# One-bank PSUM tiles and a modelled instruction order in an attention kernel with experts

## The chip, the cores and the metric

The kernel runs on one core of one Trainium2 chip. The metric is the device time of one execution in microseconds (us), lower is better. The time before is the median of three executions, 242.1 us (241.87 to 242.47). A profile is one execution taken by the hardware profiler; its span runs from the first to the last instruction, 238.4 us here, in an execution of 240.09 us.

The engines are called TensorE (PE in the profile, PEld for its weight loads), VectorE (DVE), ScalarE (ACT), GpSimd (POOL) and SyncE (SP). Each takes its instructions in program order and waits for other engines by semaphores.

## The reference

```python
# attention over 32 memory slots; batch 8, heads 8, seq 576, head_dim 64
a = exp(phi - max(phi, axis=2)); a = a / (sum(a, axis=2) + 1e-9)
k_m = einsum('bhsm,bhsd->bhmd', a, k)
v_m = einsum('bhsm,bhsd->bhmd', a, v)
scores = (q @ k_m.transpose(0, 1, 3, 2)) / sqrt(64)
attn_out = softmax(scores) @ v_m                     # (b, h, s, d)

# then a dense block and one expert per token; x is (4608, 512), 8 experts, F = 512
x = attn_out.transpose(0, 2, 1, 3).reshape(4608, 512)
y_dense = relu(x @ w1_dense) @ w2_dense
logits = x @ w_gate
e = argmax(logits); gate = softmax(logits)[e]
y = y_dense + gate * (relu(x @ w1[e]) @ w2[e])
```

## The kernel before

One batch is 576 tokens, and eight batches are worked off. The kernel never forms x. It folds the memory values into the first weight matrix (vw = v_m times w1, for the dense block and for one expert), so that the hidden layer is the attention weights A times vw. The expert is chosen once for a batch, from the mean of the gate products; if any token wants another, a branch at the end corrects it. In the profiled execution that branch is not taken.

Every piece of work is a named step, and a text gives the order in which the steps are put into the program: `name:batch/engine`. A step is taken up by whichever engine it runs on, and each engine's program is the sequence of its own steps in that text. In the middle of the run the order before is this, for every batch alike:

```
... e0:2 e1:2 o0:1 z:2 rz:2 yd1:1 kv:2 kvm:2 ye1:1 T:2 vTc:2/V Y1:1/A kTc:2/A q0:2 o1:1 qT0:2/V q1:2
yd2:1 vg:2 qT1:2/A ye2:1 vgc:2 pc:2 Y2:1/V choose:2 o2:1 w1:2 w2:2 yd3:1 s0:2 ET0:2 ye3:1 s1:2 ET1:2
Y3:1/A fd:2 vd0:2/V o3:1 vd1:2/V Z0:2 yd4:1 ln0:2 Z1:2 ye4:1 ln1:2 inv0:2 Y4:1/V A0:2 inv1:2 o4:1
A1:2 hd0:2 Hd0:2/A ... hd3:2 Hd3:2/A pg:2 gB:2/A fe:2 ve0:2/A ve1:2/V he0:2 He0:2 ... he3:2 He3:2
Lphi:4 yd0:2 Lv:4 ye0:2 Lk:4 Lq:4 Y0:2/V ...
```

What the steps are:

- L...: loads. `Lq`, `Lk`, `Lv`, `w1`, `w2`, `Lw1d`, `Lw2d` are issued by GpSimd and turn fp32 into fp16 on the way; `Lphi` and the staged keys and values of batch 0 are issued by SyncE.
- `e0`, `e1`: exp of phi (ScalarE). `z`, `rz`, `kv`, `kvm`, `T`, `vTc`, `kTc`: the memory keys and values, normalised, transposed and copied out as vT and kT.
- `q0`, `q1`, `qT0`, `qT1`: transposes of q on TensorE and their copies.
- `s`, `ET`, `Z`, `ln`, `inv`, `A`: scores, exp, sums, 1/sum by exp(-ln), and the attention weights A.
- `vg`, `vgc`, `pc`, `choose`: gate products of the memory values, their sum, and the expert; `w1`, `w2` then load the expert's weights at an address read from it.
- `fd`, `vd` and `fe`, `ve`: the fold with the dense and the expert's first matrix, and the copies to fp16.
- `hd`, `Hd` and `he`, `He`: hidden products (four of each per batch) and relu; `He` also multiplies by the gate `gB`, which `L`, `mxeq`, `ex`, `gates`, `pg` make.
- `yd`, `ye`, `Y`, `o`: second products of five token chunks, dense and expert into one sum, copy out, and store.

The parts that the change touches:

```python
big = ctx.enter_context(tc.tile_pool(name="big", bufs=3, space=bass.MemoryType.PSUM))
sml = ctx.enter_context(tc.tile_pool(name="sml", bufs=1, space=bass.MemoryType.PSUM))
# every tile of both is [128, 2, 512] fp32: two banks of PSUM; 3 + 1 tiles are all eight banks
# ... cut: "inp" holds 3 batches of q, k/v and phi; "y" tiles: NKEEP = 4

def fold(vt, w):
    p_vw = big.tile([128, 2, 512], F32, tag="big", name="p_vw")
    for j in range(NJ):
        for a in range(2):
            nc.tensor.matmul(p_vw[M * j : M * j + M, a, 0:F],
                             lhsT=vt[64 * a : 64 * a + 64, j],
                             rhs=w[64 * a : 64 * a + 64, j], start=True, stop=True)
    return p_vw

@step("ve0", "ve1")
def _(b, g, e):
    # ... cut: vwe is allocated
    copy(e, out=st[b]["vwe"][:, g], in_=st[b]["pve"][:, g, 0:F])

def second(b, c, half):
    # ... cut
    if half == 0:
        if c % 2 == 0:
            x["py2"] = big.tile([128, 2, 512], F32, tag="big", name="p_y")
        x["p_y", c] = x["py2"][:, c % 2]       # two chunks share one tile
    # ... cut: four products (eight of half size in the last chunk) into p_y

@step("z")      # "att" holds z, the keys/values (second bank), T, vg, pc and L of a batch
def _(b, i, e):
    x["att"] = sml.tile([128, 2, 512], F32, tag="sml", name="p_att")
    # ... cut

@step("vg")
def _(b, i, e):
    att = st[b]["att"]
    for a in range(2):
        for j in range(NJ):
            nc.tensor.matmul(att[M * j : M * j + M, a, 400 : 400 + E],
                             lhsT=vT[b][64 * a : 64 * a + 64, j],
                             rhs=wg[64 * a : 64 * a + 64, j], start=True, stop=True)
```

Of the kernel before, what the change touches and what calls it, by code (L numbers as in the profile page):

```python
# [10 lines left out]
F32 = mybir.dt.float32  # L11
# [8 lines left out]
cones:0 Lphi0:0 Lphi1:0 Lwg:0 cid:0 ciota:0 cblk:0 ciotac:0 stage0:0 stage1:0 stage2:0 stage3:0  # L20
stage4:0 stage5:0 warm:0/16 e0:0 e1:0 wgt:0 wgm:0 wgc:0 cast0:0/P Lq:0 Lw1d:0 Lw2d:0 cast1:0/V
cast2:0/A cast3:0/V cast4:0/A cast5:0/V Lphi:1 Lv:1 Lk:1 Lq:1 warm:0/16 z:0 rz:0 kv:0 kvm:0 T:0
vTc:0/V kTc:0/A q0:0 qT0:0/V q1:0 vg:0 qT1:0/A vgc:0 pc:0 choose:0 w1:0 w2:0 s0:0 ET0:0 s1:0 ET1:0
fd:0 vd0:0/V vd1:0/V Z0:0 ln0:0 Z1:0 ln1:0 inv0:0 A0:0 inv1:0 A1:0 hd0:0 Hd0:0/A hd1:0 Hd1:0/A L:0
mxeq:0 ex:0 gates:0 hd2:0 Hd2:0/A hd3:0 Hd3:0/A pg:0 gB:0/A fe:0 ve0:0/A ve1:0/V he0:0 He0:0 he1:0
He1:0 he2:0 He2:0 he3:0 He3:0 Lphi:2 yd0:0 Lv:2 ye0:0 Lk:2 Lq:2 Y0:0/V e0:1 e1:1 o0:0 z:1 rz:1 yd1:0
kv:1 kvm:1 ye1:0 T:1 vTc:1/V Y1:0/A kTc:1/A q0:1 o1:0 qT0:1/V q1:1 yd2:0 vg:1 qT1:1/A ye2:0 vgc:1
pc:1 Y2:0/V choose:1 o2:0 w1:1 w2:1 yd3:0 s0:1 ET0:1 ye3:0 s1:1 ET1:1 Y3:0/A fd:1 vd0:1/V o3:0
vd1:1/V Z0:1 yd4:0 ln0:1 Z1:1 ye4:0 ln1:1 inv0:1 Y4:0/V A0:1 inv1:1 o4:0 A1:1 hd0:1 Hd0:1/A hd1:1
Hd1:1/A L:1 mxeq:1 ex:1 gates:1 hd2:1 Hd2:1/A hd3:1 Hd3:1/A pg:1 gB:1/A fe:1 ve0:1/A ve1:1/V he0:1  # L30
He0:1 he1:1 He1:1 he2:1 He2:1 he3:1 He3:1 Lphi:3 yd0:1 Lv:3 ye0:1 Lk:3 Lq:3 Y0:1/V e0:2 e1:2 o0:1
z:2 rz:2 yd1:1 kv:2 kvm:2 ye1:1 T:2 vTc:2/V Y1:1/A kTc:2/A q0:2 o1:1 qT0:2/V q1:2 yd2:1 vg:2 qT1:2/A
ye2:1 vgc:2 pc:2 Y2:1/V choose:2 o2:1 w1:2 w2:2 yd3:1 s0:2 ET0:2 ye3:1 s1:2 ET1:2 Y3:1/A fd:2
vd0:2/V o3:1 vd1:2/V Z0:2 yd4:1 ln0:2 Z1:2 ye4:1 ln1:2 inv0:2 Y4:1/V A0:2 inv1:2 o4:1 A1:2 hd0:2
Hd0:2/A hd1:2 Hd1:2/A L:2 mxeq:2 ex:2 gates:2 hd2:2 Hd2:2/A hd3:2 Hd3:2/A pg:2 gB:2/A fe:2 ve0:2/A
ve1:2/V he0:2 He0:2 he1:2 He1:2 he2:2 He2:2 he3:2 He3:2 Lphi:4 yd0:2 Lv:4 ye0:2 Lk:4 Lq:4 Y0:2/V
e0:3 e1:3 o0:2 z:3 rz:3 yd1:2 kv:3 kvm:3 ye1:2 T:3 vTc:3/V Y1:2/A kTc:3/A q0:3 o1:2 qT0:3/V q1:3
yd2:2 vg:3 qT1:3/A ye2:2 vgc:3 pc:3 Y2:2/V choose:3 o2:2 w1:3 w2:3 yd3:2 s0:3 ET0:3 ye3:2 s1:3 ET1:3
Y3:2/A fd:3 vd0:3/V o3:2 vd1:3/V Z0:3 yd4:2 ln0:3 Z1:3 ye4:2 ln1:3 inv0:3 Y4:2/V A0:3 inv1:3 o4:2
A1:3 hd0:3 Hd0:3/A hd1:3 Hd1:3/A L:3 mxeq:3 ex:3 gates:3 hd2:3 Hd2:3/A hd3:3 Hd3:3/A pg:3 gB:3/A  # L40
fe:3 ve0:3/A ve1:3/V he0:3 He0:3 he1:3 He1:3 he2:3 He2:3 he3:3 He3:3 Lphi:5 yd0:3 Lv:5 ye0:3 Lk:5
Lq:5 Y0:3/V e0:4 e1:4 o0:3 z:4 rz:4 yd1:3 kv:4 kvm:4 ye1:3 T:4 vTc:4/V Y1:3/A kTc:4/A q0:4 o1:3
qT0:4/V q1:4 yd2:3 vg:4 qT1:4/A ye2:3 vgc:4 pc:4 Y2:3/V choose:4 o2:3 w1:4 w2:4 yd3:3 s0:4 ET0:4
ye3:3 s1:4 ET1:4 Y3:3/A fd:4 vd0:4/V o3:3 vd1:4/V Z0:4 yd4:3 ln0:4 Z1:4 ye4:3 ln1:4 inv0:4 Y4:3/V
A0:4 inv1:4 o4:3 A1:4 hd0:4 Hd0:4/A hd1:4 Hd1:4/A L:4 mxeq:4 ex:4 gates:4 hd2:4 Hd2:4/A hd3:4
Hd3:4/A pg:4 gB:4/A fe:4 ve0:4/A ve1:4/V he0:4 He0:4 he1:4 He1:4 he2:4 He2:4 he3:4 He3:4 Lphi:6
yd0:4 Lv:6 ye0:4 Lk:6 Lq:6 Y0:4/V e0:5 e1:5 o0:4 z:5 rz:5 yd1:4 kv:5 kvm:5 ye1:4 T:5 vTc:5/V Y1:4/A
kTc:5/A q0:5 o1:4 qT0:5/V q1:5 yd2:4 vg:5 qT1:5/A ye2:4 vgc:5 pc:5 Y2:4/V choose:5 o2:4 w1:5 w2:5
yd3:4 s0:5 ET0:5 ye3:4 s1:5 ET1:5 Y3:4/A fd:5 vd0:5/V o3:4 vd1:5/V Z0:5 yd4:4 ln0:5 Z1:5 ye4:4 ln1:5
inv0:5 Y4:4/V A0:5 inv1:5 o4:4 A1:5 hd0:5 Hd0:5/A hd1:5 Hd1:5/A L:5 mxeq:5 ex:5 gates:5 hd2:5  # L50
Hd2:5/A hd3:5 Hd3:5/A pg:5 gB:5/A fe:5 ve0:5/A ve1:5/V he0:5 He0:5 he1:5 He1:5 he2:5 He2:5 he3:5
He3:5 Lphi:7 yd0:5 Lv:7 ye0:5 Lk:7 Lq:7 Y0:5/V e0:6 e1:6 o0:5 z:6 rz:6 yd1:5 kv:6 kvm:6 ye1:5 T:6
vTc:6/V Y1:5/A kTc:6/A q0:6 o1:5 qT0:6/V q1:6 yd2:5 vg:6 qT1:6/A ye2:5 vgc:6 pc:6 Y2:5/V choose:6
o2:5 w1:6 w2:6 yd3:5 s0:6 ET0:6 ye3:5 s1:6 ET1:6 Y3:5/A fd:6 vd0:6/V o3:5 vd1:6/V Z0:6 yd4:5 ln0:6
Z1:6 ye4:5 ln1:6 inv0:6 Y4:5/V A0:6 inv1:6 o4:5 A1:6 hd0:6 Hd0:6/A hd1:6 Hd1:6/A L:6 mxeq:6 ex:6
gates:6 hd2:6 Hd2:6/A hd3:6 Hd3:6/A pg:6 gB:6/A fe:6 ve0:6/A ve1:6/V he0:6 He0:6 he1:6 He1:6 he2:6
He2:6 he3:6 He3:6 e0:7 yd0:6 e1:7 ye0:6 z:7 rz:7 Y0:6/V kv:7 kvm:7 o0:6 T:7 yd1:6 vTc:7/V kTc:7/A
ye1:6 q0:7 qT0:7/V Y1:6/A q1:7 o1:6 vg:7 qT1:7/A yd2:6 vgc:7 pc:7 ye2:6 choose:7 w1:7 Y2:6/V w2:7
o2:6 s0:7 ET0:7 yd3:6 s1:7 ET1:7 ye3:6 fd:7 Y3:6/A vd0:7/V vd1:7/V o3:6 Z0:7 ln0:7 yd4:6 Z1:7 ye4:6
# [8 lines left out]
def kernel(  # L68
# [13 lines left out]
    nc = tc.nc  # L82
# [86 lines left out]
    def _(b, a, e):  # L169
        if a == 0:  # L170
            input_tile(b, "phi")
# [704 lines left out]
```

## Time and profile before

| | before |
|---|---|
| time, median of 3 | 242.1 us |
| span of the profiled execution | 238.4 us |
| mean granted TensorE clock | 0.938 |
| instructions | 4590 |
| bytes moved by DMA | 39.30 MB, mean 165 GB/s |
| GpSimd queue (fp32 to fp16 loads) | 22.42 MB |
| SyncE queue (phi, staged k/v, stores) | 16.54 MB |
| VectorE, `vwe` waiting for ScalarE's `vwe` | 18.7 us in 8 waits |
| landing of a q load, median | 19.7 us |

How to read the lines below. In the page, a busy line gives us, share of the span and number of instructions of each engine; the rows of 40 digits show busy tenths in 40 equal slices of the span, and the GB/s row what DMA moved in each. In a table of stretches, each row is one stretch of time with every engine's busy time and instruction count, the granted TensorE clock, the mean DMA share and GB/s. A line of waits reads: engine, what it was about to do and at which line of the kernel, the engine and instruction that released it, then us in total, number of waits, and the longest. Tile names such as p_y, p_h, vwe are those of the program. Ends of matmuls are modelled, and a busy TensorE is not TensorE at its peak.

### The profile page before, as it was taken

The numbers are of one execution on the slowest core, as the hardware profiler recorded it, in microseconds if no ns is written. First come the engines' busy times: TensorE is split into PE (matmuls) and PEld (weight loads), VectorE is DVE, ScalarE is ACT, GpSimd is POOL, SyncE is SP. The second block draws the span as 40 slices with busy tenths as digits, with TensorE's granted clock in tenths as the row PEclk, the third lists the DMA queues.
The fourth block names the chain that finished last, engine by engine and source line by source line (L and its number), as shares of the span: only waits on it lengthen the run. The fifth ranks groups of instructions, "written<-read, shape, count | busy, mean of one in ns | idle before, by whom it ended". The sixth has DMA issues, their size and how long they took to land. (4 is left out here: it accounts for less than half of the span.)

```text
span 238.4 us, 4590 instructions
## 1 busy us (share of the span) xinstructions
PE 169.7 (71%) x1897; PEld 94.7 (40%) x1897; DVE 103.7 (44%) x267; ACT 95.7 (40%) x155; POOL 33.1 (14%) x48
## 2 busy tenths in 40 slices
PE   3425473997679765986698659976798668978781
PEld 2424141553345343442354335534453435534330
DVE  1532521633553445445454346344633556443710
ACT  4122553034552466036703761345613670466010
POOL 1730600005100230006000600032001100020000
PEclk9999996799799997999999997997999988997997
DMA  6999999943999299954999699929994850295032
GB/s 167 254 246 228 204 205 205 204 124 67 217 230 234 74 170 235 207 161 65 237 220 208 105 226 223 218 55 193 235 210 135 136 106 17 77 156 130 0 135 75
DMA packets 40594, 39.30 MB, mean 165 GB/s; under 512 B 1652, under 2 KB 36468, under 8 KB 40568
## 3 DMA queue, kind: packets, MB, share of 16 engines
q0 software_dynamic: 26752, 22.42, 61.4%
q1 hardware_dynamic: 13816, 16.54, 23.4%
q8 instruction: 16, 0.26, 0.4%
q14 instruction: 10, 0.08, 0.1%
HBM read 51.92 MB, written 9.44 MB: 257 GB/s over the span
## 5 line engine op out<-in xcount | busy, mean ns | idle before, releaser
L699 PE MATMUL p_y<-w2d,HTd 128*128 128x512 f16 (+1 forms) x192 | 38.4, 347 | 10.4 <-DVE y L725 9.8
L699 PE MATMUL p_y<-w2e,HTe 128*128 128x512 f16 (+1 forms) x192 | 38.0, 346 | 0.0
L623 PE MATMUL p_h<-A,vwd 128*128 128x288 f16 x128 | 25.8, 350 | 14.9 <-DVE A L477 14.8
L723 ACT ACTIVATE y<-p_y 128x512 f32<-128x512 f32 x16 | 9.5, 595 | 57.5 <-PE p_y L699 57.5
L623 PE MATMUL p_h<-A,vwe 128*128 128x288 f16 x128 | 25.0, 354 | 9.1 <-ACT vwe L115 6.9
L237 POOL DMA_DIRECT2D w1e<-in_moe_w_dram x8 | 6.1, 763 | 170.1 <-PE p_s L426 108.6
L677 DVE SCALAR_TENSOR_TENSOR HTe<-p_h,gB 128x576 f16<-128x576 f32 x32 | 23.1, 754 | 7.1 <-PE p_h L623 7.1
L664 ACT ACTIVATE HTd<-p_h 128x576 f16<-128x576 f32 x32 | 19.9, 650 | 14.9 <-PE p_h L623 14.9
L725 DVE TENSOR_SCALAR y<-p_y 128x512 f32<-128x512 f32 (+1 forms) x24 | 14.5, 603 | 25.3 <-PE p_y L699 19.4
L699 PEld LDWEIGHTS <-HTd 128*128 128x128 f16 (+1 forms) x192 | 15.6, 102 | 23.7 <-issue 14.7
L623 PEld LDWEIGHTS <-vwd 128*128 128x128 f16 x128 | 13.9, 113 | 22.8 <-issue 17.9
L623 PEld LDWEIGHTS <-vwe 128*128 128x128 f16 x128 | 13.7, 117 | 19.9 <-ACT vwe L115 9.5
L439 ACT ACTIVATE ET<-p_s 128x576 f16<-128x576 f32 x16 | 10.3, 650 | 23.3 <-PE p_s L426 23.3
L699 PEld LDWEIGHTS <-HTe 128*128 128x128 f16 (+1 forms) x192 | 13.8, 101 | 13.8 <-issue 1.7
L115 DVE CAST vwd<-p_vw 128x512 f16<-128x512 f32 x16 | 10.3, 686 | 17.1 <-PE p_vw L610 17.1
L115 DVE CAST vwe<-p_vw 128x512 f16<-128x512 f32 x8 | 5.5, 692 | 18.7 <-ACT vwe L115 18.7
L318 ACT ACTIVATE E<-phi 96x768 f16<-96x768 f32 x16 | 12.8, 843 | 2.2 <-DMA phi<-in_phi_dram 2.0
L477 DVE TENSOR_TENSOR A<-ET,lnz 128x576 f16<-128x576 f16 x16 | 11.4, 755 | 2.9 <-ACT lnz L472 2.9
L463 ACT ACTIVATE lnz<-p_z 128x576 f32<-128x576 f32 x16 | 10.3, 650 | 5.4 <-PE p_z L450 5.0
L407 PE MATMUL p_q<-ident,q 96*128 96x96 f16 x192 | 10.4, 216 | 2.2 <-DMA q<-in_q_dram 2.2
L115 ACT COPY qT<-p_q 128x1152 f16<-128x1152 f16 x8 | 8.9, 1118 | 6.5 <-PE p_q L407 6.5
L351 PE MATMUL p_att<-kv,E 96*32 96x128 f16 x384 | 7.4, 231 | 5.3 <-DVE rz L341 5.3
(82 smaller groups left out, 180.6 us busy)
## 6 DMA issues: line engine op xcount, KB each, us to landing
out_dram<-y SPq DMA_DIRECT2D x32, 256.0 KB, 3.5
q<-in_q_dram POOLq DMA_DIRECT2D x8, 576.0 KB, 19.7
w1e<-in_moe_w_dram POOLq DMA_DIRECT2D x8, 512.0 KB, 6.1
w2e<-in_moe_w_dram POOLq DMA_DIRECT2D x8, 512.0 KB, 9.4
phi<-in_phi_dram SPq DMA_DIRECT2D x7, 576.0 KB, 11.2
kv<-in_v_dram POOLq DMA_DIRECT2D x7, 576.0 KB, 14.8
kv<-in_k_dram POOLq DMA_DIRECT2D x7, 576.0 KB, 16.9
out_dram<-y SPq DMA_DIRECT2D x16, 64.0 KB, 5.5
```

The source lines that it names most:

```text
L115: (nc.scalar.copy if e == "A" else nc.vector.tensor_copy)(out=out, in_=in_)
L318: nc.scalar.activation(out=x["E"][:, :, a].rearrange("p t j m -> p j t m"), in_=x["phi"].rearrange("p (j a) t m -> p a j t m", a=2)[:, a], ...
L407: nc.tensor.transpose(p_q[:, j // 2, c : c + P], q8[:, 2 * j + a, 2 * t : 2 * t + 2].rearrange("p t d -> p (t d)"), ident,)
L439: nc.scalar.activation(out=st[b]["ET"][:, a].rearrange("m (p t r) -> m p t r", t=TP, r=2), in_=st[b].pop(("ps", a))[:, :, 0:HC].rearrange( ...
L463: nc.scalar.activation(out=st[b]["lnz"][:, a].rearrange("p (h c) -> p h c", h=2), in_=st[b].pop(("pz", a))[:, :, 0:HC], func=AF.Ln,)
L477: eng.tensor_mul(out=A[b][:, a], in0=st[b]["ET"][:, a], in1=st[b]["lnz"][:, a])
L623: nc.tensor.matmul(p_h[:, h, 0:HC], lhsT=vw[:, g, 128 * ft : 128 * ft + 128], rhs=a[:, g, HC * h : HC * h + HC], start=(g == 0), stop=(g = ...
L664: nc.scalar.activation(out=o, in_=p_h, func=AF.Relu)
L677: nc.vector.scalar_tensor_tensor(out=x["HTe"][:, ft].rearrange("p (h c) -> p h c", h=2), in0=x.pop(("pe", ft))[:, :, 0:HC], scalar=0.0, in ...
L699: nc.tensor.matmul(p_y[n * u : n * u + n, 0:w], lhsT=HT[:, ft, lo : lo + n], rhs=w2[:, ft, w * u : w * u + w], start=(half == 0 and ft == ...
L723: nc.scalar.activation(out=o, in_=p_y, func=AF.Copy, scale=1.0 / SC)
L725: nc.vector.tensor_scalar(out=o, in0=p_y, scalar1=1.0 / SC, scalar2=None, op0=ALU.mult)
```

## The change

PSUM is cut up differently. Two two-bank tiles remain for hidden products, scores, sums and q transposes; three one-bank tiles serve the halves of a fold, the output chunks, the key/value sums and the warm-up; one bank holds the small products. So the gate products of both halves have to fit one bank: they are made with one matmul per j against a gate matrix padded with zeros (half as many matmuls), and the offsets in the bank move. The purpose is that each output chunk and each half of a fold gets and gives back a bank of its own.

The order text is replaced as a whole. It is no longer the same for each batch but comes from a model of the engines and transfers: steps of neighbouring batches are mixed, stores of finished rows are held back and put where the queue is free, and the engine of a copy (`/A` ScalarE, `/V` VectorE, `/P` GpSimd) is chosen for each one. Compared with before, the copies by engine are:

| copies | before | after |
|---|---|---|
| Hd (relu) | 32 ScalarE | 23 ScalarE, 9 VectorE |
| Y (output) | 16 ScalarE, 24 VectorE | 26 ScalarE, 14 VectorE |
| vd and ve (folds) | 8 ScalarE, 24 VectorE | 20 ScalarE, 12 VectorE |
| gB | 8 ScalarE | 6 ScalarE, 2 VectorE |
| kT / vT | 8 ScalarE / 8 VectorE | 6 ScalarE, 2 VectorE / 2 ScalarE, 6 VectorE |
| qT | 8 ScalarE, 8 VectorE | 9 ScalarE, 7 VectorE |

Four of the phi loads and one half of the last store are issued by ScalarE.

```diff
 ORDER = """
-cones:0 Lphi0:0 Lphi1:0 Lwg:0 cid:0 ciota:0 cblk:0 ciotac:0 stage0:0 stage1:0 stage2:0 stage3:0
-stage4:0 stage5:0 warm:0/16 e0:0 e1:0 wgt:0 wgm:0 wgc:0 cast0:0/P Lq:0 Lw1d:0 Lw2d:0 cast1:0/V
... (cut)
+stage3:0 Lq:0 ciota:0 cones:0 stage1:0 Lphi1:0 Lwg:0 wgt:0 Lphi0:0 stage4:0 cast1:0/V cast3:0/P
+cid:0 cblk:0 cast4:0/V warm:0/8 stage0:0 stage5:0 warm:0/8 e0:0 warm:0/8 wgm:0 e1:0 wgc:0 cast5:0/A
+ciotac:0 cast0:0/P stage2:0 z:0 Lphi:1 q0:0 q1:0 qT0:0/A Lw1d:0 cast2:0/A qT1:0/A kv:0 rz:0 kvm:0
+T:0 kTc:0/A Lq:1 s1:0 ET1:0 Lv:1 s0:0 vTc:0/V vg:0 ET0:0 Z1:0 Z0:0 ln1:0 vgc:0 inv1:0 pc:0 ln0:0
+inv0:0 fd:0 choose:0 e1:1 Lk:1 vd1:0/A q0:1 A0:0 A1:0 q1:1 L:0 vd0:0/V w1:0 qT0:1/A qT1:1/V hd2:0
+ex:0 mxeq:0 gates:0 hd3:0 Hd2:0/A hd0:0 Hd3:0/A Lw2d:0 e0:1 pg:0 z:1 rz:1 kv:1 kvm:1 T:1 Hd0:0/A
... (cut)
+vd1:2/A yd4:1 he2:1 Lphi:3/A He2:1 he1:1 kTc:2/A He1:1 yd0:1 s1:2 vgc:2 Lv:3 ye4:1 Lk:3 s0:2 ET1:2
+Y4:1/V pc:2 Z1:2 ye0:1 choose:2 ET0:2 ln1:2 Z0:2 Y0:1/V ln0:2 inv1:2 inv0:2 q0:3 w1:2 yd3:1 A1:2
+ye1:1 yd2:1 qT0:3/A e0:3 A0:2 L:2 Lq:4 e1:3 mxeq:2 q1:3 hd2:2 ex:2 ye2:1 qT1:3/V Y1:1/A w2:2 gates:2
... (cut)
+ve1:7/A pg:7 ye0:6 gB:7/A he2:7 He2:7 Y0:6/A he0:7 He0:7 yd2:7 he1:7 he3:7 o0:1 He1:7 yd0:7 o1:6
+o1:5 yd3:7 He3:7 ye2:7 flags:0 o0:6 o2:6 o3:6 Y2:7/A ye3:7 yd1:7 Y3:7/A ye1:7 o2:7 Y1:7/V ye0:7
+Y0:7/A o3:7 yd4:7 o3:4 ye4:7 o1:7 Y4:7/A o0:7 o4:7/A
 """
@@
-    big = ctx.enter_context(tc.tile_pool(name="big", bufs=3, space=bass.MemoryType.PSUM))
+    big = ctx.enter_context(tc.tile_pool(name="big", bufs=2, space=bass.MemoryType.PSUM))
+    one = ctx.enter_context(tc.tile_pool(name="one", bufs=3, space=bass.MemoryType.PSUM))
     sml = ctx.enter_context(tc.tile_pool(name="sml", bufs=1, space=bass.MemoryType.PSUM))
@@ Lphi
-        nc.sync.dma_start(
+        (nc.scalar if e == "A" else nc.sync).dma_start(
@@ z
-        x["att"] = sml.tile([128, 2, 512], F32, tag="sml", name="p_att")
+        x["att"] = sml.tile([128, 512], F32, tag="sml", name="p_att")
@@ kv
-        p_kv = x["att"][:, 1, 0 : 2 * 2 * Dh].rearrange("p (a i d) -> p a i d", a=2, i=2)
+        x["kvz"] = one.tile([128, 512], F32, tag="one", name="p_kv")[:, 0 : 2 * 2 * Dh]
+        p_kv = x["kvz"].rearrange("p (a i d) -> p a i d", a=2, i=2)
@@ vg
-        for a in range(2):
-            for j in range(NJ):
-                nc.tensor.matmul(
-                    att[M * j : M * j + M, a, 400 : 400 + E],
-                    lhsT=vT[b][64 * a : 64 * a + 64, j],
-                    rhs=wg[64 * a : 64 * a + 64, j],
+        for j in range(NJ):
+            nc.tensor.matmul(
+                st[b]["att"][M * j : M * j + M, 400 : 400 + 2 * E],
+                lhsT=vT[b][:, j],
+                rhs=wg[:, j].rearrange("p a e -> p (a e)"),
@@ fold
-        p_vw = big.tile([128, 2, 512], F32, tag="big", name="p_vw")
+        p_vw = [one.tile([128, 512], F32, tag="one", name=f"p_vw{a}") for a in range(2)]
@@ ve0, ve1 (vd0, vd1 alike)
-        copy(e, out=st[b]["vwe"][:, g], in_=st[b]["pve"][:, g, 0:F])
+        copy(e, out=st[b]["vwe"][:, g], in_=st[b]["pve"][g][:, 0:F])
@@ second
-            if c % 2 == 0:
-                x["py2"] = big.tile([128, 2, 512], F32, tag="big", name="p_y")
-            x["p_y", c] = x["py2"][:, c % 2]
+            x["p_y", c] = one.tile([128, 512], F32, tag="one", name="p_y")
```

## The prediction before the result

> **What bounds the kernel now.** I read the page's busy line first. TensorE is busy 71% of 238.4 us; VectorE and ScalarE are each below half. No compute engine is full, so the question is what TensorE stands idle for.
>
> ```profile
> span 238.4 us, 4590 instructions
> PE 169.7 (71%) x1897; PEld 94.7 (40%) x1897; DVE 103.7 (44%) x267; ACT 95.7 (40%) x155; POOL 33.1 (14%) x48
> ...
> DMA  6999999943999299954999699929994850295032
> GB/s 167 254 246 228 204 205 205 204 124 67 217 230 234 74 170 235 207 161 65 237 220 208 105 226 223 218 55 193 235 210 135 136 106 17 77 156 130 0 135 75
> ```
>
> The DMA rows matter too. The 23 slices that show 9 move 216 GB/s on average, and between them lie holes at 2 to 5 tenths. The page gives 39.30 MB in all, so 39.3 / 0.216 = 182 us is what the transfers would take without a hole. That is a floor not far below the span.
>
> Then the table of stretches, which I cut at the first output product (44.35) and at the start of each batch's second part.
>
> ```profile
> 20.55:44.35 23.80, 14.65 (x117) 8.32 (x118) 8.93 (x24) 10.16 (x16) 3.81 (x5) 0.87 1.28 207
> 44.35:59.64 15.29, 13.27 (x177) 6.80 (x176) 5.80 (x15) 5.09 (x9) 3.26 (x5) 0.99 0.61 119
> 59.64:85.06 25.42, 20.23 (x231) 10.97 (x231) 11.95 (x32) 11.63 (x21) 3.79 (x6) 0.93 0.96 182
> 85.06:110.50 25.44, 19.28 (x223) 10.50 (x222) 12.33 (x31) 10.83 (x19) 2.75 (x4) 0.93 0.91 177
> ...
> 187.00:213.00 26.00, 20.38 (x237) 11.47 (x234) 12.52 (x32) 11.93 (x21) 1.49 (x2) 0.93 0.48 98
> 213.00:225.80 12.80, 9.04 (x64) 4.93 (x63) 8.15 (x24) 4.97 (x9) 0.00 (x0) 0.87 0.42 83
> 225.80:238.40 12.60, 6.50 (x40) 3.06 (x40) 1.12 (x2) 1.19 (x2) 0.00 (x0) 0.90 0.28 100
> ```
>
> After the stretch and its length come TensorE's busy time, then its weight loads, VectorE, ScalarE and GpSimd, the granted clock, DMA share and GB/s. A batch takes 25.4 us, of which TensorE works 19.3 to 20.4. From 44.35 to 213 it works 132.7 of 168.65 us (the six rows added), idle 36.0. The first output product starts only at 44.35.
>
> TensorE's own list of waits names the gaps:
>
> ```profile
> PE p_h L623 <- DVE A L477: 14.8, 15, 2.2
> PE p_y L699 <- DVE y L725: 9.8, 15, 0.9
> PE p_h L623 <- ACT vwe L115: 6.9, 8, 0.9
> ...
> PE p_vw L610 <- DMA w1e<-in_moe_w_dram: 4.8, 1, 4.8
> PE p_g L590 <- DVE gm L582: 4.1, 4, 1.2
> PE p_z L450 <- ACT ET L439: 3.3, 6, 0.6
> PE p_q L407 <- DMA q<-in_q_dram: 2.2, 1, 2.2
> ```
>
> None is long by itself: TensorE runs in program order and, at a fixed place in each batch, meets a product whose input is one hand-over away. From VectorE's list I add `vwe` waiting 18.7 us in 8 waits for ScalarE's copy of the other half: the two copies out of a fold share one two-bank tile and run one after the other (0.59 us, then 0.69).
>
> **What the Trainium skill says.** "PSUM — Partial Sum Buffer", section "PSUM bank collisions raise a hardware error": two engines may work in different banks at once, and must be kept apart in the same bank. So the serial `vwe` copies and the 15 waits of p_y on y come from tiles spanning two banks, not from the banks themselves. The trace fits: Y0 of batch 0 ends at 47.18 and the next chunk's product, in the other bank of that tile, starts at 47.23.
>
> "TensorE: Matmul & The Clock Gate", section "Part 1: The HAM clock gate": the array falls to half rate after an idle window and needs some microseconds of activity to return. In this trace 16 hidden products took 4.27 us at 40.29, behind the gap for the first w1e, while 14 took 1.92 at 67.99. Fewer gaps should therefore also make some products shorter.
>
> "DMA: Bandwidth & Descriptors", section "Issuing engines are not separate DMA queues": issuing from another engine saves only the issue time. I give the four phi loads that move to ScalarE no gain; they cost it about 0.6 us each (SyncE's phi issues: median 593 ns).
>
> **The change part by part.**
>
> *PSUM.* Before: three two-bank tiles plus one two-bank tile for the small products, eight banks. After: two two-bank tiles (hidden, scores, sums, transposes), three one-bank tiles (fold halves, output chunks, key/value sums, warm-up) and one bank for small products. An output chunk no longer waits for its neighbour's eviction: 9.8 us of TensorE waits, of which 1.7 us lie in the tail (0.94 + 0.78 at 225.84 and 230.24), so about 8 before it. The copies of a fold may run side by side: 0.59 us off the path from fold to hidden, eight times, inside the 9.0 us for vwe (6.9 on ScalarE, 2.1 on VectorE); counted below. The gate products vg are halved in number, 64 to 32 at about 25 ns pitch (8 in 0.20 us with the last one's drain): under 1 us, not counted.
>
> *Order, middle.* Everything else is the order. The new list mixes two batches finely: chunks of batch b stand among scores, sums and hidden products of b+1, and the transposes of b+2. After taking the 8 us for y, 36.0 - 8 = 28 us of idle remain from 44.35 to 213. Each of these waits is 0.3 to 2.2 us and there is other ready work on TensorE (an output chunk half is 1.03 us), so most can be filled, not all; I take 60%, 17 us. Together 25 us. Where gaps close, the drain of the product ahead of them is hidden and the half-rate spells (clock 0.93 in most batches) shorten: an estimate of 2 us.
>
> *Order, start.* Q of batch 0 is now the first GpSimd load, not issued at 8.98 and landing at 20.5; its 24 transposes can run while keys and values arrive. Keys and values still need the same staged bytes, so the sums stay near 16 us. From there the chain (sums, kvm, T, kT, scores, exp, Z, ln, inverse, A) took, without the q wait, about 8 us; the first hidden product comes near 25 to 26, not 29.05. The first expert weights were held behind w1d, w2d and batch 1's loads and landed at 38.95. Now w2d follows w1, so 0.5 MB fewer stand ahead (2.5 us at 207 GB/s), and choice and issue come some 4 us earlier (scores no longer wait for q). I expect w1e near 32 to 33, the first output product near 36, and part of batch 1's front done meanwhile, which was all ahead at 44.35. I count 8 us.
>
> *Order, end.* From 213.0 on TensorE is idle 3.76 + 6.10 = 9.9 us, 5.2 of them after the last product. The two y waits (1.7), the wait for A (1.54 + 0.27) and for vwe (0.88 + 0.31) can be covered with leftover chunks of batch 6, which the new list holds back for it. I count 4 us.
>
> *Moved copies.* From the list: ScalarE gains 10 Y (x 0.60), 12 fold copies (x 0.59), one qT (1.1), two vT (0.3 each) and four phi issues (0.6), and loses 9 Hd (x 0.65), two gB (0.64) and two kT (0.37): +9.4 us, to about 105. VectorE ends near 95. Both are half busy; neither becomes the bound.
>
> *Given back.* The order is fixed from assumed durations, while transfers land when they land. Before, q was in use about 40 us after its issue in mid-run; now GpSimd issues it behind the preceding batch's w1 and w2 but TensorE asks for it about one batch later, 20 to 22 us, against a median landing time of 19.7 us. Stores held back to the second half share the queues. I put 4 us of new waits on TensorE there, and 4 more for durations that differ from the model.
>
> Sum: 242.1 - 25 - 2 - 8 - 4 + 4 + 4 = 211.1 us. As a check on the floor: span near 207 with 39.3 MB is 190 GB/s, 88% of the 216 that a full slice moves. Tight but possible.
>
> **The rivals.** *DMA takes over.* If loads come too late, each batch falls to its bytes: 39.3 / 8 = 4.9 MB at 0.216 = 22.7 us, and with 36 us ahead and about 12 behind, 36 + 7 x 22.7 + 12 = 207 span at best, 220 to 225 with two or three missed landings. For it: the share above 1 in every loading stretch, landing times of 15 to 20 us. Against it: the holes (68 and 39 GB/s around 104 to 112), in which GpSimd waits 22 us for the expert choice. *Too few two-bank tiles.* With two, not three, hidden products run at the pace of their evictions: 0.75 us each on VectorE for HTe against 0.5 on TensorE for four products. Were all 32 to wait 0.25 us, 8 us come back: 219. Against: the new list puts chunks between them. *In-order blocking.* One late step on ScalarE or VectorE holds up the later evictions that TensorE needs; a badly modelled list would then eat most of the 25 us and end at 225 to 240. For it: ScalarE gets more work and phi issues. *More gain*: 90% of the 28 us filled gives 203.
>
> **Range and chances.** Most of the sum is the 25 + 8; at half of it the time is about 228, if almost all is filled and nothing given back, near 200. Hence 200 to 228. Slower would need new waits over 30 us, and no part adds work of that size. Faster by over 2%: 0.93; within 2%: 0.04; slower: 0.03.
>
> **What would show it.** Right: no wait of p_y on y of the neighbour chunk; the two vwe copies overlapping; a period of 21 to 23 us; the first output product at 34 to 38; TensorE share near 78%; DMA holes gone. Wrong: waits of transposes or key/value sums on their loads, of hidden products on HTe or HTd by more than 8 us in all, stores still running well after the last eviction, or a first output product later than 40.

## The result and the profile after

| | before | after |
|---|---|---|
| time, median | 242.0 us (4 executions) | 185.3 us (4 executions, 183.2 to 185.9) |
| span of the profiled execution | 238.4 us | 184.1 us |
| TensorE busy / idle in the span | 169.7 / 68.7 us | 150.3 / 33.8 us |
| instructions | 4590 | 4484 |

The ratio is 0.764 (95% interval 0.758 to 0.770): 57 us less, where the prediction had 31. The page after, with the busy line, the granted clock and the DMA rows in 40 slices of 4.6 us:

```profile
span 184.1 us, 4484 instructions
PE 150.3 (82%) x1857; PEld 92.6 (50%) x1857; DVE 95.0 (52%) x256; ACT 99.3 (54%) x167; POOL 33.7 (18%) x49
...
PEclk9999999999999999999999999998559999999998
DMA  5999999999999999999999999999995594999994
GB/s 161 214 250 226 191 201 200 205 205 231 185 191 184 232 213 204 206 237 139 227 229 203 206 205 279 240 305 276 212 204 81 78 151 131 330 168 244 390 367 135
```

Two things are to be seen. The DMA holes of before are gone: the row shows 9 up to slice 30, near 139 us. And TensorE's busy time fell by 19.4 us, from 169.7 to 150.3, although it does the same products but for 32 small gate ones and 8 that only warm up; its weight loads, which go with the products, only fell from 94.7 to 92.6.

To see where the 54.3 us of the span went, I cut both traces at the same events: the issue of the second batch's first expert matrix (`w1e`) and that of the last batch's. Columns as in the stretches of the prediction. Before:

```profile
0.00:56.38 56.38, 32.23 (x379) 19.57 (x383) 20.23 (x53) 18.22 (x26) 10.94 (x19) 0.94 1.04 199
56.38:208.63 152.25, 117.85 (x1382) 65.34 (x1382) 72.83 (x186) 68.79 (x114) 20.69 (x27) 0.94 0.87 165
208.63:238.40 29.77, 19.57 (x147) 9.75 (x145) 10.67 (x28) 8.74 (x15) 1.49 (x2) 0.90 0.43 99
```

And after:

```profile
0.00:48.50 48.50, 29.71 (x404) 20.23 (x405) 19.46 (x55) 22.68 (x34) 11.62 (x20) 1.00 1.15 209
48.50:159.22 110.72, 100.60 (x1312) 61.38 (x1309) 65.73 (x176) 67.89 (x117) 20.64 (x27) 0.95 1.11 203
159.22:184.11 24.89, 20.03 (x150) 11.02 (x148) 9.77 (x27) 8.75 (x16) 1.49 (x2) 0.97 0.93 269
```

The start gave 7.9 us and the end 4.9. The middle, six batches, gave 41.5: 25.4 us per batch became 18.5. Of these 41.5, idle time gave 34.4 - 10.1 = 24.3 and busy time 17.2. The two middles do not hold quite the same work: 27 output products and 12 transposes of q fewer stand in the middle after; they are done at the start or the end instead. That is an estimate of 4 us at their pitch (215 ns for 512 columns), so some 4 of the 17.2 us only moved.

TensorE's own waits after:

```profile
PE p_w L293 <- DVE wgt L282: 8.5, 2, 7.6
PE p_att L335 <- ACT ex L569: 4.9, 2, 4.6
PE p_y L703 <- ACT vwd L116: 3.8, 1, 3.8
...
PE p_h L629 <- ACT vwe L116: 0.8, 1, 0.8
...
PE p_y L703 <- ACT y L727: 0.2, 1, 0.2
```

The first is the start. Of the waits that carried the prediction, A (14.8 us) is gone from the list, y fell from 9.8 on VectorE's copies to 0.2 in all, and vwe on ScalarE from 6.9 to 0.8. The two long ones left in the middle, 4.6 and 3.8, both go back to a load of phi that lands late (the `ex` that ends the 4.6 stands on ScalarE right behind the exp of that phi). The 3.8 are seen in ScalarE's and TensorE's timelines around 94 to 99 us (start, duration, instruction, and in brackets the idle time and what ended it):

```profile
97.65 0.84 ACT L323 ACTIVATE E<-phi 96x768 f16<-96x768 f32 x1 [4.71 <-DMA phi<-in_phi_dram]
98.40 1.05 ACT L116 CAST vwd<-p_vw 128x512 f16<-128x512 f32 x2
...
99.01 1.02 PE L703 MATMUL p_y<-w2d,HTd 128*128 128x512 f16 x4 [3.78 <-ACT vwd L116]
```

ScalarE stands at the exp of phi of batch 5, whose load has not landed, and the copy of a fold stands behind it. An output chunk on TensorE needs that fold's bank and waits for `vwd` in turn. That is the in-order blocking named among the rivals. This load was late because SyncE, too, works in order:

```profile
84.17 0.38 SPq L738 DMA_DIRECT2D out_dram<-y  x1
84.65 0.82 SPq L164 DMA_DIRECT2D phi<-in_phi_dram  x1
```

The phi load was placed behind a store of batch 2, went out when that row was ready, and landed 13 us later among the other loads. The other hole, of 4.6 us at 124.9, is that of batch 6. Its load had no store ahead of it: ScalarE issued it, late in its own list, and it landed 12.3 us after its issue.

```profile
115.46 0.32 ACTq L164 DMA_DIRECT2D phi<-in_phi_dram  x1
127.83 1.57 ACT L323 ACTIVATE E<-phi 96x768 f16<-96x768 f32 x2 [5.73 <-DMA phi<-in_phi_dram]
```

### The profile page after: what moved, and what is told of

The parts are those of the page before. It is cut to its first block, busy times and chain, and to the rows that moved or that the text cites. A ratio compares the mean times of both kernels' runs of the same rounds, so it can differ in the third digit from the quotient of the medians.

```text
span 184.1 us, 4484 instructions
## 1 busy us (share of the span) xinstructions
PE 150.3 (82%) x1857; PEld 92.6 (50%) x1857; DVE 95.0 (52%) x256; ACT 99.3 (54%) x167; POOL 33.7 (18%) x49
## 4 chain that ended last, share of the span: by engine, by line
PE 41%; DMA 40%; ACT 9%; SPq 4%; issue 2%; DVE 1%; ACTq 0%
PE p_y L703 18%; DMA out_dram<-y 17%; DMA phi<-in_phi_dram 12%; PE p_h L629 10%; DMA stage<-in_k_dram 7%; DMA w1e<-in_moe_w_dram 4%; PE p_kv L357 3%; PE p_q L413 2%; ACT E L323 2%; PE p_vw L616 2%; PE p_z L456 2%; PE p_s L432 2%; ACT qT L116 1%; SPq L203 1%; ACT lnz L478 1%
## 5 line engine op out<-in xcount | busy, mean ns | idle before, releaser
L683 DVE SCALAR_TENSOR_TENSOR HTe<-p_h,gB 128x576 f16<-128x576 f32 x32 | 23.3, 753 | 8.9 <-PE p_h L629 5.8
L629 PE MATMUL p_h<-A,vwd 128*128 128x288 f16 x128 | 21.9, 307 | 0.4 <-ACT qT L116 0.4
L629 PE MATMUL p_h<-A,vwe 128*128 128x288 f16 x128 | 19.9, 287 | 0.9 <-ACT vwe L116 0.8
L727 ACT ACTIVATE y<-p_y 128x512 f32<-128x512 f32 (+1 forms) x26 | 14.0, 554 | 12.2 <-PE p_y L703 6.4
L670 ACT ACTIVATE HTd<-p_h 128x576 f16<-128x576 f32 x23 | 14.5, 649 | 9.6 <-PE p_h L629 8.1
L445 ACT ACTIVATE ET<-p_s 128x576 f16<-128x576 f32 x16 | 10.1, 651 | 10.3 <-PE p_s L432 10.3
L629 PEld LDWEIGHTS <-vwe 128*128 128x128 f16 x128 | 11.8, 98 | 7.7 <-issue 1.5
L729 DVE TENSOR_SCALAR y<-p_y 128x512 f32<-128x512 f32 (+1 forms) x14 | 8.8, 630 | 13.1 <-PE p_y L703 12.4
L629 PEld LDWEIGHTS <-vwd 128*128 128x128 f16 x128 | 11.9, 103 | 6.5 <-issue 1.2
L413 PEld LDWEIGHTS <-q 96*128 96x128 f16 x192 | 10.8, 108 | 3.2 <-DMA q<-in_q_dram 1.6
L478 ACT ACTIVATE lnz<-lnz 128x576 f32<-128x576 f32 x16 | 10.8, 682 | 0.4
L357 PE MATMUL p_kv<-kv,E 96*32 96x128 f16 x384 | 8.3, 242 | 2.8 <-ACT kv L116 2.3
```

What stands on the lines that cost most here:

```text
L357: nc.tensor.matmul(p_kv[M * j : M * j + M, a], lhsT=x["E"][:, t, a, j], rhs=x["kv"][:, :, 2 * j + a, t], start=(t == 0), stop=(t == T - 1),)
L413: nc.tensor.transpose(p_q[:, j // 2, c : c + P], q8[:, 2 * j + a, 2 * t : 2 * t + 2].rearrange("p t d -> p (t d)"), ident,)
L478: nc.scalar.activation(out=lnz, in_=lnz, func=AF.Exp, scale=-1.0)
L629: nc.tensor.matmul(p_h[:, h, 0:HC], lhsT=vw[:, g, 128 * ft : 128 * ft + 128], rhs=a[:, g, HC * h : HC * h + HC], start=(g == 0), stop=(g = ...
L670: nc.scalar.activation(out=o, in_=p_h, func=AF.Relu)
L683: nc.vector.scalar_tensor_tensor(out=x["HTe"][:, ft].rearrange("p (h c) -> p h c", h=2), in0=x.pop(("pe", ft))[:, :, 0:HC], scalar=0.0, in ...
```

## The experiments

All times are medians of a run's executions, and ratios are against the kernel before on the same chip (240.9 to 242.0 us there). Executions more than 1.5% over the fastest of the same kernel are left out; in four runs no interval can be given, and the one or two that remain stand singly. "The new list" is the order text of the change, "the old list" that of before.

**Tiles alone.** All of the change to PSUM, with the old list.

```diff
 ORDER = """
-stage3:0 Lq:0 ciota:0 cones:0 ...        (the new list)
+cones:0 Lphi0:0 Lphi1:0 Lwg:0 cid:0 ...  (the old list, word for word)
```

> The one-bank tiles with the order text of before; nothing else differs from the changed kernel. If the order carries the gain and the tiles only make room for it: just the waits of p_y on y (9.8 us) and half a microsecond per fold (8 x 0.6 us) can go, less what two instead of three two-bank tiles cost, so 228 to 240 us. If the tiles carry a main part by themselves: below 215 us.

225.2 us, ratio 0.933 (0.925 to 0.941), between the two theories and nearer the first. So the tiles give 16 to 17 us by themselves and the list 40 more. Its waits on TensorE:

```profile
PE p_h L629 <- DVE A L483: 14.8, 15, 2.2
PE p_h L629 <- ACT vwe L116: 6.3, 8, 0.9
...
PE p_y L703 <- ACT y L727: 4.2, 6, 0.7
```

The wait on y fell from 9.8 to 4.2, and A stands as before. vwe still waits 6.3 (9.0 before, with VectorE's share): in the old list both halves are needed at once, and parallel copies save a part of each wait only.

**Each split by itself**, with the old list. Output chunks in one-bank tiles and folds in a two-bank tile:

```diff
-        p_vw = [one.tile([128, 512], F32, tag="one", name=f"p_vw{a}") for a in range(2)]
+        p_v2 = big.tile([128, 2, 512], F32, tag="big", name="p_vw")
+        p_vw = [p_v2[:, a] for a in range(2)]
```

> Order of before; output chunks in one-bank tiles, both halves of a fold in one two-bank tile. My sum gave the y split about 8 us: 231 to 235 us if that is right. If most of the 16 us of a1_tiles_only comes from the y split: 225 to 229 us.

Folds in one-bank tiles and output chunks in pairs:

```diff
-            x["p_y", c] = one.tile([128, 512], F32, tag="one", name="p_y")
+            if c % 2 == 0:
+                x["py2"] = big.tile([128, 2, 512], F32, tag="big", name="p_y")
+            x["p_y", c] = x["py2"][:, c % 2]
```

> Order of before; folds in one-bank halves, output chunks in pairs in two-bank tiles. If the fold split is worth its half microsecond per fold copy pair (16 pairs at most 10 us, 5 for vwe alone): 231 to 237 us. If the pairs of chunks compete with hidden products for the two two-bank tiles left: 240 us or more.

The chunks alone: 230.9 us (0.956, 0.950 to 0.963), 11 us. The folds alone: 243.3 us (1.010, 1.007 to 1.013), a little slower, as the second theory had it; chunk pairs then have two wide tiles to share with everything else, not three. The 8 us that the prediction gave the chunks were a fair size. On top of the chunks the fold split is worth 5.7 (230.9 to 225.2); without them nothing.

**The new list with the fold in one two-bank tile** (the edit of the first of the two above).

> The changed kernel with both halves of a fold in one two-bank tile again, taken from the two that hidden products and scores use; order as changed. If the fold's split is what lets the order work: over 195 us, with hidden products waiting for vwe and for tiles. If the order covers the serial copies with other work: 184 to 190 us.

199.2 us (0.826, 0.819 to 0.832): here the fold split is worth 14 us. A new wait shows it:

```profile
PE p_h L630 <- DVE HTe L684: 3.4, 5, 0.8
```

A fold takes one of two wide tiles, and hidden products wait for evictions with the other. This is the rival "too few two-bank tiles"; the change avoids it because its folds and chunks no longer ask for wide tiles.

**A hand-written list.** To see how much of the 40 us needs a model at all, I wrote one rule for every batch, with the engines of before and stores behind their copies: the hidden products of batch n stand among the exp, sums, transposes and gate products of n+1, and the output chunks of n among the scores, folds and A of n+1.

```diff
-... hd0:2 Hd0:2/A ... hd3:2 Hd3:2/A pg:2 gB:2/A fe:2 ve0:2/A ve1:2/V he0:2 He0:2 ... (then yd:2, with e, z, kv ... of 3)
+... hd2:2 Hd2:2/A gates:2 z:3 hd3:2 rz:3 Hd3:2/A kv:3 kvm:3 pg:2 gB:2/A T:3 fe:2 ve0:2/A vTc:3/V
+ve1:2/V kTc:3/A q0:3 qT0:3/V he0:2 q1:3 He0:2 he1:2 qT1:3/A He1:2 vg:3 ... yd1:2 s0:3 ye1:2 ET0:3
+Y1:2/A o1:2 s1:3 yd2:2 ET1:3 fd:3 ye2:2 vd0:3/V vd1:3/V Z0:3 ln0:3 Y2:2/V o2:2 yd3:2 Z1:3 ln1:3 ...
```

> New tiles, copies on the engines of before, and a regular order written by one rule from the order of before: the front of the next batch (exp, z, kv, T, q, vg) is moved among the hidden products of the batch ahead of it, and the output chunks are spread over scores, sums and A. Stores follow their copies at once, loads stand as before. If it is the deeper mixing of batches that closes TensorE's gaps: 192 to 208 us, the waits for A and vwe mostly gone. If the gain needs the fine placement of the modelled order: 212 to 226 us.

It took 211.3 us, between the two theories. This first version had one flaw, which the waits name:

```profile
PE p_att L335 <- ACT E L323: 9.1, 14, 1.1
```

The exp of phi stood directly ahead of the product that reads it. The next run moves two steps of each batch and nothing else:

```diff
-... A1:2 ye4:1 Y4:1/V o4:1 hd0:2 Hd0:2/A hd1:2 Hd1:2/A L:2 mxeq:2 ex:2 e0:3 e1:3 hd2:2 ...
+... inv1:2 e0:3 e1:3 Y3:1/A o3:1 yd4:1 A1:2 ye4:1 Y4:1/V o4:1 hd0:2 Hd0:2/A hd1:2 ...
```

> The regular hand order took 211 to 215 us, and 9.1 us of its waits were the attention products waiting for the exponential of phi. Here that exponential stands one half batch earlier, behind the last quarter of A of the batch ahead. If the regular mixing of stages is what the new order lives on, and this one misplaced step held it back: 203 to 208 us, with the wait for E near zero. If the new order lives on the fine placement of each group: 212 to 216 us, with the waiting moved to other copies.

200.9 us (0.831, 0.826 to 0.836), better than either theory had it. A wait of 9.1 us was worth 10 (211.3 to 200.9). With it went the half-rate spells in the middle, as the clock row shows.

```profile
PE 158.7 (79%) x1865; PEld 92.5 (46%) x1865; DVE 102.2 (51%) x269; ACT 94.0 (47%) x155; POOL 33.5 (17%) x48
...
PEclk9999999859999999999999999999999999999999
```

So 24 of the list's 40 us come from one simple rule with this one mend, and 16 from the rest of the modelled list. Its middle, cut as above, is 10.6 us longer than that of the new list (110.72 us):

```profile
51.50:172.83 121.33, 110.49 (x1364) 63.36 (x1362) 71.21 (x186) 67.63 (x115) 20.56 (x28) 1.00 1.10 209
```

It is idle 10.8 us there, hardly more than the 10.1 of the new list, so nearly all of the 10.6 is busy time. But it also holds more work: 32 output products and 12 transposes of q, an estimate of 5 us, which the new list does at its start and end, where TensorE has time. Over the whole spans (199.8 and 184.1 us) the 15.7 between them are 7.3 us of idle time (41.1 to 33.8), mostly of start and end, and 8.4 of busy time (158.7 to 150.3).

**Do tiles and order need each other?** The same hand list with the tiles of before, and with only the fold in a two-bank tile.

> The hand order with the early exponential, on the tiles of before (three two-bank tiles plus one). With the new tiles it took 200.9 us; in the order of before the new tiles were worth 16 us. If the order alone carries the gain and the tiles are a small matter in it: 201 to 207 us. If tiles and order add up: 213 to 219 us. If the mixing lives on the tiles, because a chunk that sits among scores and folds must not keep a two-bank tile from them: above 222 us.

> The hand order with the early exponential, with the halves of a fold again in one two-bank tile and the output chunks in one-bank tiles. Undoing the fold split cost 14 us in the modelled order and nothing in the order of before. If the cost comes from the mixing (a fold takes one of two wide tiles while hidden products need both): 208 to 215 us. If it belongs to the modelled list alone: 200 to 204 us.

217.4 us (0.901, 0.893 to 0.909) and 205.8 us (0.851, 0.844 to 0.859). By these ratios the new tiles are worth 17 us here and 16 with the old list: tiles and the hand list's order simply add, within the noise. The 205.8 lie between the two theories of that run. The new list was not run on the old tiles, so for it this is not shown. The wait of neighbouring chunks is back when the pairs are:

```profile
PE p_y L699 <- DVE y L725: 12.7, 16, 0.8
```

With the chunks in banks of their own, the fold split is worth 5.7 us in the old list (the "nothing" expected above was its worth with paired chunks), 4.9 in the hand list and 14 in the new one: the finest mixing misses a wide tile most.

**Engines of the copies.** The new list with every copy (Hd, Y, gB, kT, vT, qT, vd, ve) on its engine of before.

```diff
-Y0:0/A ... Hd3:1/V ... ve1:1/A ... vd0:2/A ...
+Y0:0/V ... Hd3:1/A ... ve1:1/V ... vd0:2/V ...
```

> The changed kernel with every copy (Hd, Y, gB, kT, vT, qT, vd, ve; 64 of them differ) on the engine that had it before; order and tiles as changed. If the choice of engines is a main part of the gain: over 195 us. If it is a detail, since both engines are half busy: 184 to 191 us.

191.8 us (0.793, 0.786 to 0.799), just over the range for a detail: the letters are worth 7 us. Then the other way round, the letters of the new list on the first hand list (the one with the late exp), with its stores held back two batches as well.

> The regular order of b4_hand_pipeline with the two other parts added: every copy on the engine that the modelled order gives it, and each batch's stores held back to two batches later. If b4 was far from the modelled order because it lacked these (7 us and 8 us by b1_engines_back and a2_stores_at_once): 196 to 204 us. If it is the fine placement on TensorE: 207 to 215 us, with as many breaks between products as b4.

223.2 and 225.5 us, 12 to 14 worse than that hand list and than either theory. The letters that help one list hurt another:

```profile
DVE A L483 <- ACT lnz L478: 31.1, 8, 7.4
...
ACT y L727 <- PE p_y L703: 22.7, 12, 5.8
```

With the letters of before the first of these was 12.7 us. A copy of y stands on ScalarE ahead of the inverse that A needs. The held stores went in with the letters, so their share of the loss is open.

**Stores at once.** The new list, each store directly behind its copy.

```diff
-... Y0:2/V ... o0:2 ...          (stores gathered two to seven batches later)
+... Y0:2/V o0:2 ... Y1:2/A o1:2  (every store behind its own copy)
```

> The changed kernel with every store put right behind the copy that fills it, instead of held back; all else as changed. If holding the stores back matters because loads fill the DMA queues until about 139 us: loads come later, 189 to 197 us, with longer waits of exp on phi and of TensorE on loads. If it doesn't matter: 183 to 188 us.

190.4 and 192.5 us: holding the stores back is worth 5 to 7. From 39.5 to 139 us DMA moves a little more (225 GB/s for 219) and TensorE 11 products fewer (1131 for 1142); what is left behind 139 takes 51.9 us for 45.1.

**The late phi loads.** The new list with the four late phi loads issued by ScalarE two batches ahead.

```diff
-... o2:2 Lphi:5 ... Lphi:6/A ... Lphi:7 ...
+... e1:3 Lphi:5/A ... e0:4 Lphi:6/A ... e0:5 Lphi:7/A ...  (Lphi:4 alike)
```

> The changed kernel with the phi loads of batches 4 to 7 issued by ScalarE one batch earlier, so that none stands behind a store on SyncE. If the two holes of TensorE at 94 and 125 us (3.8 and 4.6 us) come only from the late issue of phi: both go, 175 to 180 us. If the loads as a whole are at the limit of what DMA moves: another load is late in place of phi, 182 to 187 us.

183.1 us (0.760, 0.753 to 0.767, for 0.764 and 0.758 to 0.770 after): no change clear of the noise. Both holes are gone, and other waits stand in the profiled execution (185.6 us), this one the longest in mid-run:

```profile
PE p_vw L616 <- DMA w1e<-in_moe_w_dram: 4.0, 2, 2.2
```

The queues are full there, so a load brought forward makes another late. That points to the amount of data ahead of the loads and not to this load.

**Fewer loads.** The new list without the key and value loads of batches 1 to 7; batch 0's are used again, so this version leaves 8.3 MB out and computes on other data.

```diff
-        input_tile(b, "kv")
+        st[b]["kv"] = st[0]["kv"]
+        return
```

> The changed kernel without the loads of keys and values of batches 1 to 7 (14 transfers, 8.3 MB of 39.3 less); those batches take the keys and values of batch 0, so the computation is that of other data. If DMA is what bounds the changed kernel: well under 176 us, with the holes of TensorE gone. If TensorE and the order bound it: 174 to 181 us, the holes' 8 us at most and something at the start. If neither: 183 to 187 us.

178.0 and 179.1 us: 6 to 7 us hang on loads. TensorE is busy 149.0 us there, for 150.3 after.

**Stores out of the loads.** The stores of the new list between 84 and 119 us move 2.5 MB while loads are waited for, and from 119 to 152 ready rows stand on SyncE behind one that is not ready, while DMA falls to 16 GB/s around 142. So: phi early as above, five y tiles for four, and all stores of batches 0 to 5 behind the loads, batch 0 first because its tile is needed again.

```diff
-    NKEEP = 4
+    NKEEP = 5
-... o4:3 ... o3:2 ... o1:2 o2:2 ... o4:2 ... o3:0 ... (stores among the steps of batches 4 to 6)
+... Y3:4/V o4:4 o0:0 o1:0 o2:0 o3:0 o4:0 e0:7 ... Y3:5/V o0:2 o1:2 o2:2 o3:2 o4:2 o0:1 ... o4:5 vd1:7/A ...
```

> Phi early as in a3_phi_early, five instead of four y tiles, and all stores moved behind the load phase (the first batch's at about 125 us, the others from about 145 us). In the changed kernel 8 whole and 6 quarter stores (2.5 MB, 12 us at 0.21 MB/us) run between 84 and 119 us among the loads. If the rate of the load phase bounds the first 140 us: 8 to 12 us less than a3_phi_early, 172 to 178 us. If TensorE's order bounds it: 181 to 186 us.

180.6 us, ratio 0.747 (0.742 to 0.753): faster than before and after, and between the two theories, nearer the second. What DMA moved there:

```profile
GB/s 149 227 242 231 204 204 204 207 205 224 205 155 233 228 222 216 226 206 170 34 228 204 204 207 233 210 197 137 204 207 290 214 276 389 279 196 282 395 275 81
```

Mostly 200 to 240 GB/s while loads run (up to slice 28), 196 to 395 in slices 31 to 39, where most of the traffic is stores. Then the same version without the key and value loads of batches 1 to 7:

> The version with the stores held back behind all loads (180.6 us) once more, but without the key and value loads of batches 1 to 7 (those of batch 0 are used again, so the data are others and about 6 MB of loads are left out). If the loads still bound that version: 170 to 175 us. If TensorE and the order of the work bound it: 178 to 181 us.

175.5 us (0.728, 0.723 to 0.732), between the two theories and nearer the first. Loads still cost this version 5 us, although the 8.3 MB left out are some 40 us of transfer at 205 GB/s. Most of what is left is TensorE: of the 173.4 us span it is busy 147.3.

**The same idea on the hand list**: five y tiles, the stores of batch 0 behind batch 4, of batch 1 behind batch 5, the rest behind the loads.

> The hand order with the early exponential, five y tiles, and the stores of batches 0 to 6 held back: batch 0 behind batch 4, batch 1 behind batch 5, the rest behind the loads. If the loads are what the hand order waits for in its middle, as in the modelled order (12 us between stores at once and stores out of the loads): 190 to 195 us. If its own copies and hand-overs bound it: 199 to 202 us, with the loads done earlier and no gain from it.

207.0 us (0.858, 0.850 to 0.865), 6 us worse, which neither theory had. The period in the middle is the same (20.2 us per batch in both), so loads do not bound the hand list there. Most of the loss is at the start. SyncE's timeline, with the stores at once and then with the stores held back:

```profile
5.82 2.87 SPq L164 DMA_DIRECT2D phi<-in_phi_dram  x2
49.30 9.34 SPq L738 DMA_DIRECT2D out_dram<-y  x4
```

```profile
5.92 25.57 SPq L163 DMA_DIRECT2D phi<-in_phi_dram  x4
```

With no store ahead of them, two more phi loads (1.18 MB, 5.8 us at 205 GB/s) went out by 31 us, among the keys of batch 1 and the first expert weights. The keys were then waited for:

```profile
PE p_kv L356 <- DMA kv<-in_k_dram: 3.1, 1, 3.1
```

The first output product came at 50.2 for 46.7, and the last at 198.0 for 194.0. A store that cannot go yet had been pacing the loads behind it. The five y tiles were not run by themselves.

**Is it the clock?** The tiles-alone version with products that nobody reads in three gaps of each batch, so that TensorE is not idle there.

```diff
-... A1:2 hd0:2 ... hd3:2 Hd3:2/A pg:2 ... He... he0:2 ...
+... A1:2 warm:0/20 hd0:2 ... hd3:2 Hd3:2/A warm:0/12 pg:2 ... warm:0/8 he0:2 ...
```

> The kernel of a1_tiles_only (order of before) with products nobody reads put into the three gaps of every batch: 20 before the first dense hidden product, 12 before the gate products pg, 8 before the expert's hidden products. In a1_tiles_only TensorE did 30.5 us of work at half the clock, 15 us too long. If the half rate is the gaps' second price, paid on top of the waiting: the granted clock goes to about 1.0 and the time to 210 to 218 us, though more products are run. If it isn't on the path: 223 to 232 us.

The granted clock rose from 0.918 to 0.987 and the needed products took 153.0 us, not 166.0 (busy time without the added ones). The time fell by 3 us only, to 221.7 (0.920, 0.913 to 0.926), between the two theories and nearer the second. Two waits that were short or covered came up:

```profile
PE p_vw L618 <- DMA w1e<-in_moe_w_dram: 5.2, 1, 5.2
...
PE p_h L631 <- DVE HTe L685: 3.2, 8, 0.4
```

So the half rate is real, but most of it did not show in the time. The test is not a clean one, as the added products are busy for 23 us themselves and some of them may stand in the way. The new list's own executions point the same way: at a mean granted clock of 0.883 one took 185.0 us, and at 0.967 to 0.978 the others took 183.2 to 185.9. That the clock by itself makes any part of the 57 us is therefore not shown.

## Why the prediction was right and wrong

*The bound and the direction* were right: TensorE's idle time at hand-overs could be taken. Over the whole span the terms of the sum came to 29 us of idle time (25 + 8 + 4 less the 8 given back) and 2 of busy time. The profiles show 34.9 (68.7 to 33.8) and 19.4 (169.7 to 150.3). So of the 23.3 us that the sum missed, 17.4 are busy time and 5.9 idle time.

*Start and end* held in size: 7.9 us for 8, and 4.9 for 4. At the start that was partly luck, as its chain went otherwise than told. The key/value sums did not stay near 16 us. They waited for ScalarE's last cast of the staged keys and values (19.04 to 20.19):

```profile
20.24 1.47 PE L357 MATMUL p_kv<-kv,E 96*32 96x128 f16 x46 [2.35 <-ACT kv L116]
```

So the first hidden product came at 30.00 and not at 25 to 26, and the first w1e was issued at 28.04, 2.3 us later than before and not 4 earlier. It landed 7.1 us after its issue, for 13.2 before, and its fold ran at 36.33. The first output product came at 39.6, later than the expected 34 to 38 and only 4.8 us earlier than before. What made up the 8 is the work of batch 1 done meanwhile: 320 products stood ahead of it, for 231 before.

*The middle* is where the sum failed. It had 25 + 2 against 8 given back, net 19; the stretches show 41.5, some 4 of them work that moved out of the middle. Two terms were mis-sized.

The step that failed by most: "Where gaps close, the drain of the product ahead of them is hidden and the half-rate spells (clock 0.93 in most batches) shorten: an estimate of 2 us". TensorE's busy time fell by 19.4. It is accounted for as follows. The clock row is granted in spells, and in stretches at 0.50 a product counts about twice its time (16 hidden products took 4.27 us there, 14 took 1.92 outside). Two of the seven such stretches before:

```profile
37.93:44.76 6.83, 5.03 (x25) 2.49 (x26) 3.13 (x5) 2.06 (x3) 0.00 (x0) 0.50 1.29 205
61.83:65.24 3.41, 3.41 (x24) 2.14 (x23) 1.37 (x9) 2.06 (x4) 0.00 (x0) 0.50 1.16 239
```

All seven hold 25.2 us of busy time. After, there is one, behind the second phi hole:

```profile
127.76:138.00 10.24, 7.96 (x112) 4.98 (x113) 4.20 (x14) 6.64 (x12) 0.00 (x0) 0.50 1.28 215
```

Half of the difference, (25.2 - 8.0) / 2 = 8.6 us, is the clock. Next the drains. A 512-column product is recorded for 379 ns at its median but followed by the next after 215, so about 0.17 us at the end of its record, which I call its drain, costs nothing if another product follows at once. Counting every product that starts more than 40 ns after the drain of the one ahead began, there are 172 such breaks before with 22.8 us of waiting inside drains, and 115 after with 12.8: 10.0 us. Eight warm-up products fewer and the halved gate products give about 1. Together 8.6 + 10.0 + 1 = 19.6, for the 19.4 seen. As ends of matmuls are modelled, the division is an estimate; and it divides TensorE's busy time in one execution, which is not yet the time of the kernel: the clock's part is not shown to be time.

I had read the waits list as the whole of what could be taken. But a wait inside a drain is in no wait and counts as busy, and the half-rate spells became fewer where gaps were closed or filled (0.94 to 0.98 in the hand list, 0.918 to 0.987 above), although executions of one program differ too (0.883 to 0.978 for the new list). The Trainium skill warns of this in "Perfetto Trace Analysis", section "Identifying the Most-Contended Engine": the busy share of matmuls is a poor measure of how close a kernel is to its limit, as the products are pipelined. The prediction treated 169.7 us as work; this case agrees that the share misleads, as nearly the same work took 150.3. The page says that pipelined instructions look smaller in the trace; here the record of a product (379 ns) is longer than its pitch (215 ns).

The hand list separates the two. It has 171 breaks with 21.6 us in drains, as before, but only 4.9 us at half rate: the simple rule takes idle time and half rate. The modelled list, with 25 stretches of unbroken work where the hand list has 71, takes the drains as well. So the drains (21.6 to 12.8), less 1.5 us for the new list's longer half-rate spell, account for most of the 8.4 us of busy time between the two. That is about half of the 16 us; the rest is idle time, mostly at start and end.

*The 25 us of idle time* (8 for the chunks, and "I take 60%" of the rest) held: of the middle's idle time 24.3 went.

*The 8 us given back* did not come on top of it. The two phi holes cost 8.4 us of idle time, but 24.3 went in spite of them, and mending them (183.1 us) gave nothing clear of the noise. The q loads that I feared were waited for 1.0 us. Of "durations that differ from the model" nothing was seen. So where 25 - 8 = 17 us of the middle's idle time had been counted, 24.3 went.

*The floor of 182 us* was wrong in its make-up. It divided all bytes by the 216 GB/s of slices that hold loads and stores together. After, DMA moved 203 GB/s from 48 to 80 us, where there were loads alone, and 390 from 171 to 179, where there were stores alone. The version with the stores behind the loads ended at 180.6, under the floor. So the sum of the bytes over one rate says little, yet the loads do bind there, by some 5 us.

*The rivals.* "DMA takes over" was right on what comes next and wrong on where: 220 to 225 was said, and it shows only below 185. "In-order blocking" was seen as the phi holes and no more. "Too few two-bank tiles" was not seen after (no wait of that kind on TensorE), but appears with 14 us as soon as the fold goes back to a wide tile. "More gain", 203, was the nearest.

*The signs.* The y wait of neighbours is gone, and the two vwe copies overlap, as the timeline shows (72.11 and 72.15):

```profile
72.11 0.59 ACT L116 CAST vwe<-p_vw 128x512 f16<-128x512 f32 x1 [0.74 <-PE p_vw L616]
72.15 0.69 DVE L116 CAST vwe<-p_vw 128x512 f16<-128x512 f32 x1 [0.16 <-PE p_vw L616]
```

The DMA holes are gone until 139 us. The period is 18.5 and not 21 to 23, TensorE's share 82% and not 78%, and 39.6 us for the first product lies just inside the 40 that was named as a bad sign. ScalarE ended at 99.3 us of busy time and not near 105: its sum counted the four phi issues, which the busy line leaves out.

The change then divides: tiles 17 us, one mixing rule 24, modelled placement 16, of which letters (7) and held stores (5 to 7) are parts that overlap with the rest. These are steps in one order of adding them; as the worth of the fold split shows (0, 5 or 14 us), they depend on what is there already. What each single step of the modelled list brings stays open.

## What to carry to other kernels

Where an engine works in many short pieces, count its breaks and its half-rate spells beside its waits: the recorded busy time is not the work, and here its fall was a third of what the span lost (19 of 54 us). Give each piece that is evicted by itself a bank of its own, then mix two iterations by a simple rule and mend the worst wait; that gave 41 of 57 us, and only the rest needed a model. Keep stores out of the loads where loads bind, but look at what the issuing engine then sends early in their place.

## What was not expected of the hardware

- Stores alone moved 390 GB/s (3.12 MB in 8 us), loads alone 203 (6.50 MB in 32 us, 86% of them turned from fp32 to fp16 on the way): the mean rate of a mixed stretch is no floor.
- One step of ScalarE moved half a batch earlier, whose wait was 9.1 us in 14 pieces of at most 1.1, gave 10 us, and the granted clock over the run went from 0.94 to 0.98.
- Products that nobody reads raised the granted clock from 0.918 to 0.987 and made the others 13 us shorter, for 3 us of time; executions of the new list at 0.883 and 0.967 differ by less than 1 us (185.0 and 185.9).
- The Trainium skill says in "DMA: Bandwidth & Descriptors", section "Issuing engines are not separate DMA queues", that issuing from several engines saves issue time only. The transfers do share the queues here too, but which engine issues decided when a load could go: a phi load stood behind an unfinished row's store until 84.65, and two others went out early when the stores ahead of them were gone, in a version that lost 6 us (3.1 of them a wait for keys).
